# Spectral mixing with the operands swapped for modes 48 to 59

## The chip, the cores and the metric

The kernel runs on one core of a Trainium2 chip. The metric is the time of one execution on the device in microseconds. Before the change it is 430.06 us (median of 3 runs, 429.33 to 431.21). A trace of one execution is read with it; that execution took 429.86 us, with 427.9 us from its first to its last instruction.

## The reference, cut to what matters

Two stages follow each other. The first is causal attention in a sliding window of 64 over 8 batches, 8 heads, 576 positions and a head size of 64. Its output `x` has the shape 8 x 576 x 512. The second is a spectral mix:

```python
X = np.fft.rfft(x, axis=1)
Xr, Xi = np.real(X[:, :64]), np.imag(X[:, :64])
Yr = np.einsum('bmd,mde->bme', Xr, w_r) - np.einsum('bmd,mde->bme', Xi, w_i)
Yi = np.einsum('bmd,mde->bme', Xr, w_i) + np.einsum('bmd,mde->bme', Xi, w_r)
Y[:, :64] = Yr + 1j * Yi
u = x + np.fft.irfft(Y, n=576, axis=1)
return u + np.maximum(u @ w_ch, 0.0)
```

Each of the 64 modes has two weight matrices of 512 x 512 float32, 128 matrices in all. They are by far the largest input: each is 1 MB in memory.

## The kernel before, in words

**Attention** (to about 147 us in the trace) runs batch by batch. At the end of each batch a DFT by matmul (`dft`) and a turn (`dft_turn`, lines 345 to 353) put the spectrum into the tile `XQ`. Line 352 copies real and imaginary part, line 353 the negative of the imaginary part.

**Mixing** goes through 127 *halves*, numbered 0 to 126. A half is one weight matrix of one mode: real or imaginary (mode 0 has only the real one). `half(i)` does half i. The weight matrix is the standing operand: for each of four output blocks `e` and four input blocks `c`, a block of 128 x 128 weights is loaded into the array, and 16 columns of the spectrum (8 batches, real and imaginary) move past it. That is 16 matmuls of 16 columns, all on line 551:

```python
nc.tensor.matmul(out=view(psy, off + 2 * B * e, [[1, 2 * B]]),
                 lhsT=w[:, c, 128 * e:128 * e + 128],
                 rhs=XQ[:, m // HM, c, :, 1 - im:3 - im, m % HM], ...)
```

The result stands with the channels on the partitions, which is what the later stages need. Eight modes share one of two PSUM banks `psy`; after the eighth, two copies (VectorE on line 59, ScalarE on line 58) bring them to `YT` (modes 0 to 47) or `YTl` (modes 48 to 63).

**Weights** are loaded by `load_w` (line 125) from POOL's queue, 512 KB in bfloat16 each. At most eight transfers are in flight. The places for them form `ring`; `issue(i)` runs after half i and starts as many loads as `ring` and the count `places` allow. `taken` books places that other tiles need for a time, and `put(i, f, delta)` hangs a piece of work `f` behind half i and books `delta` places from there.

**The order** is written out by hand, half by half, for all compute engines. Behind halves 33 to 94 hangs the channel matmul of `x` (lines 681 to 695: transposes, `psz`, `Z0`). Behind halves 95 to 120 (from S_I = 95) hangs the inverse transform of modes 0 to 47: for each batch a turn of `YT` (`psa`, line 718, copied on line 719) and a channel matmul (`psw`, line 724, copied on line 726), then, through `first_rows` (line 733), `add_z` (`pse`, line 743) and `make_u` (`psf`, line 757), which VectorE adds to `Z0` and to `x`; and `last_tile` (`psg`). All these use float32r operands. Behind halves 120 to 124 stand five matmuls each (`psd`, line 815) whose result nobody reads. The end, after half 126, adds modes 48 to 63 (lines 882 to 922), rectifies, and stores the output.

Of the kernel before, what the change touches and what calls it, by code (L numbers as in the profile page):

```python
# [10 lines left out]
FP32R = mybir.dt.float32r  # L11
BF16 = mybir.dt.bfloat16
# [8 lines left out]
def view(ap, off, dims):  # L21

    return bass.AP(ap.tensor, ap.offset + off, [list(ap.ap[0])] + [list(d) for d in dims])
# [3 lines left out]
def kernel(  # L27
# [10 lines left out]
    nc = tc.nc  # L38
    B, H, S, D = q.shape
    NM = moe_w_r.shape[0]  # L40
# [5 lines left out]
    NC = DM // 128  # L46
# [8 lines left out]
    def evac(o, i, on_act):  # L55

        if on_act:
            return nc.scalar.copy(out=o, in_=i)  # L58
        return nc.vector.tensor_copy(out=o, in_=i)  # L59
# [5 lines left out]
    xqp = wl.enter_context(tc.tile_pool(name="xqp", bufs=1))  # L65
# [4 lines left out]
    ident_r = consts.tile([128, 128], FP32R, name="ident_r")  # L70
    trigF = consts.tile([128, NT, 2 * NM], BF16, name="trigF")
    x_sb = keep.tile([128, B // 2, 2 * NT, DM], BF16, name="x_sb")
    HM = NM // 2
    XQ = xqp.tile([128, 2, NC, B, 3, HM], BF16, name="XQ")

    def block(b, t):

# [36 lines left out]
    NLOAD = 2 * NM - 1  # L114
# [5 lines left out]
    def load_w(i, pool, tag, wt=None):  # L120
        m, im = divmod(i + (i > 0), 2)
        if wt is None:
            wt = pool.tile([128, NC, DM], BF16, name="wt", tag=tag)
        src = moe_w_i if im else moe_w_r
        nc.gpsimd.dma_start(out=wt, in_=src[m].rearrange("(p c) e -> p c e", c=NC))  # L125
        wtiles[m, im] = wt
# [28 lines left out]
    with tc.tile_pool(name="tmpf", bufs=1, side="right") as tmp:  # L155
# [6 lines left out]
        for t0, t1 in ((0, 3), (3, NT)):  # L162
            n = t1 - t0
# [14 lines left out]
    for i in range(4):  # L178
        half = i % 2
        pp = slice(64 * (i // 2), 64 * (i // 2) + 64)  # L180
        own = band[pp, half, 64 * half:64 * half + 64]
# [77 lines left out]
    for half in range(2):  # L259
        pp = slice(64 * half, 64 * half + 64)  # L260
        nc.vector.tensor_copy(out=band2[pp], in_=band[pp, half, :])
# [83 lines left out]
    def dft_turn(b):  # L345
        ps = ps_misc.tile([128, NC, 2, NM], BF16, name="pxq", tag="misc")
        for c in range(NC):
            nc.tensor.transpose(out=ps[:, c, :, :].rearrange("p r m -> p (r m)"), in_=Xs[b][:, c, :],
                                identity=ident_bf)
        for h in range(2):  # L350
            mm = slice(HM * h, HM * h + HM)
            nc.vector.tensor_copy(out=XQ[:, h, :, b, 1:3, :], in_=ps[:, :, :, mm])
            nc.scalar.mul(out=XQ[:, h, :, b, 0, :], in_=ps[:, :, 1, mm], mul=-1.0)

    nw = 0
    EARLY = LW + EW
# [42 lines left out]
    with tc.manual_schedule(engines={mybir.EngineType.PE, mybir.EngineType.Pool}):  # L399
# [11 lines left out]
        for b in range(1, B):  # L411
            start = -(-9 * (b - 1) // 2)
# [12 lines left out]

        for w in range(NWIN + 1):
            todo = [lambda b=b: dft_turn(b) for b in turns]
            turns[:] = dfts
            todo += [lambda b=b: dft(b) for b in dfts]
            dfts.clear()  # L430
            todo += [lambda b=b, j=j: unit(b, j) for b, j in sched.get(w, [])]
            n = len(todo)
# [16 lines left out]
            if w in (NWIN - 4, NWIN - 1):  # L449
                i = (B - 2) % 2 if w == NWIN - 4 else (B - 1) % 2  # L450
                spare(kTs[i])
                spare(qtp.tile([128, 4, S], BF16, name="qT"))
            if w in (NWIN - 4, NWIN):
                i = (B - 2) % 2 if w == NWIN - 4 else (B - 1) % 2
# [4 lines left out]
        for b in turns:  # L459
            dft_turn(b)  # L460
# [10 lines left out]
    MG = 8  # L471
    E0 = 96
    L0 = E0 // (2 * MG)
    R = 128 - E0
# [7 lines left out]
    YT = late.tile([128, B, NC, E0], FP32R, name="YT")  # L482
    YTl = late.tile([128, NC, B, R], FP32R, name="YTl")
# [9 lines left out]
    psys = [ps_y.tile([128, DM], FP32, name=f"psy{i}") for i in range(2)]  # L493
# [4 lines left out]
    ring.append((VT0, wlow, "wo", None))  # L498
    ring.append((2 * HM - 2, None, None, view(XQ, 0, [[DM, NC], [1, DM]])))

    Z_I = 33
    S_I = 2 * L0 * MG - 1
    T_I = NLOAD - 2
    work = {}
    taken = [0] * (NLOAD + 1)

    def put(i, f, delta=0):
        work.setdefault(i, []).append(f)
        for j in range(i, NLOAD + 1):
            taken[j] += delta  # L510

    def issue(i):
        nonlocal nw
        while nw < NLOAD:
            ring.sort(key=lambda r: (max(r[0], i), r[1] is not None, r[0]))
            if ring[0][0] > i:
                return
            if ring[0][1] is None and nw > S_I:
                first_u.append(ring.pop(0)[3])
                for j in range(i, NLOAD + 1):  # L520
                    taken[j] += 1
                continue
            held = [r[0] for r in ring if r[0] > i] + [nw]
            if any(sum(x > j for x in held) + taken[j] > places for j in range(i, nw + 1)):
                return
            _, pool, tag, ap = ring.pop(0)
            load_w(nw, pool, tag, ap)
            ring.append((nw, pool, tag, ap))
            nw += 1
# [10 lines left out]
    def give(c):  # L540
        ring.append((now, *c[1][1:]))

    def half(i):
        m, im = divmod(i + (i > 0), 2)
        w = wtiles.pop((m, im))
        psy = psys[m // MG % 2 if m < NM - 1 else 0]
        off = (m % MG) * NC * 2 * B if m < NM - 1 else 0
        own = m % MG == 0 or m == NM - 1
        for e in range(NC):
            for c in range(NC):  # L550
                nc.tensor.matmul(out=view(psy, off + 2 * B * e, [[1, 2 * B]]),  # L551
                                 lhsT=w[:, c, 128 * e:128 * e + 128],
                                 rhs=XQ[:, m // HM, c, :, 1 - im:3 - im, m % HM],
                                 start=own and not im and e == 0 and c == 0,
                                 stop=c == NC - 1 and (im == 1 or m == 0), skip_group_check=True)
        if (im or not m) and (m % MG == MG - 1 or m == NM - 2):
            g, n = m // MG, m % MG + 1
            for ri in range(2 if m < NM - 1 else 0):
                if g < L0:
                    dst = view(YT, g * 2 * MG + ri * MG, [[E0, NC], [NC * E0, B], [1, n]])  # L560
                else:
                    dst = view(YTl, (g - L0) * 2 * MG + ri * MG, [[B * R, NC], [R, B], [1, n]])
                evac(dst, view(psy, ri, [[2 * B, NC], [2, B], [NC * 2 * B, n]]), ri)

    class Parts:

# [99 lines left out]
    xts = []  # L666
# [2 lines left out]
        xts.extend(claim("xT") for _ in range(2))  # L669

    def drop_xts():
        for c in xts:
            give(c)

# [27 lines left out]
    put(Z_I, take_xts, 2)  # L702
    for k, f in enumerate(pieces):
        put(Z_I + k * (S_I - Z_I) // len(pieces), f)
    put(S_I - 1, drop_xts, -2)


    Yp, U = {}, {}
# [109 lines left out]
    with tc.manual_schedule(engines={E.PE, E.Pool, E.DVE, E.Activation}):  # L818
        with ExitStack() as pz:
            for now in range(S_I):  # L820
                if now == Z_I - 1:
                    late3 = p2.enter_context(tc.tile_pool(name="late3", bufs=1, side="right", reuse_waits="tile"))
                    Z0 = late3.tile([128, NS, 2, DM], FP32R, name="Z0")
                    ps_t = pz.enter_context(tc.tile_pool(name="ps_t", bufs=2, space=PSUM, reuse_waits="tile"))
                    ps_z = pz.enter_context(tc.tile_pool(name="ps_z", bufs=2, space=PSUM, reuse_waits="tile"))
                half(now)
                issue(now)
                if now == LW + 2:
                    nc.gpsimd.dma_start(out=wch, in_=moe_w_ch.rearrange("(c p) e -> p c e", p=128))
                if now == Z_I + 2:  # L830
                    for p in range(NP):
                        nc.gpsimd.tensor_copy(out=x_sb[64:128, p, NT - 1, :], in_=x_sb[0:64, p, NT, :])
                for f in work.get(now, []):
                    f()
        with ExitStack() as pe:
            ps_a = pe.enter_context(tc.tile_pool(name="ps_a", bufs=1, space=PSUM, reuse_waits="tile"))
            ps_e = pe.enter_context(tc.tile_pool(name="ps_e", bufs=2, space=PSUM, reuse_waits="tile"))
            for now in range(S_I, T_I):
                half(now)
                issue(now)  # L840
                for f in work.get(now, []):
                    f()
                if now >= T_I - 5:
                    psd = ps_e.tile([128, 2, DM], FP32, name="psd", tag="pse")
                    idle(psd[:, 0, :], 5)
# [48 lines left out]
        def turn(h, pw, pt):  # L894
            yl = [view(YTl, (e * B + 4 * h) * R, [[1, 128]]) for e in range(NC)]
            for e in range(NC):
                nc.tensor.matmul(out=pw, lhsT=yl[e], rhs=wch[:, e, :],
                                 start=(e == 0), stop=(e == NC - 1), skip_group_check=True)
            for e in range(NC):
                nc.tensor.transpose(out=pt[:, 128 * e:128 * e + 128].bitcast(FP32R), in_=yl[e], identity=ident_r)  # L900
# [27 lines left out]
        for k in range(6):  # L928
# [6 lines left out]
        half(T_I + 1)  # L935
        idle(bank(2, 1), 2)
        nc.vector.tensor_copy(out=view(YTl, 3 * MG - 1, [[B * R, NC], [R, B], [MG, 2]]),
                              in_=view(psys[0], 0, [[2 * B, NC], [2, B], [1, 2]]))
        turn(0, psys[1], psys[0])
        idle(bank(2, 1), 2)  # L940
        nc.scalar.copy(out=YY[0][:, 0, :], in_=psys[1])
# [55 lines left out]
```

## Time and profile before

| | |
|---|---|
| Median of 3 runs | 430.06 us (429.33 to 431.21) |
| The profiled execution | 429.86 us, span 427.9 us |
| TensorE busy | 355.8 us (83%), 5151 matmuls |
| L551, half matmuls | 1744 rows, 68.0 us busy, 192 ns each |
| VectorE, ScalarE, GpSimd busy | 199.9, 150.7, 91.4 us |
| Mean granted TensorE clock | 0.794 |
| DMA from POOL's queue | 81.80 MB, 96.0% of 16 engines' span |
| Loads of weights | 512 KB each, 19.1 us from issue to landing (median) |

A row of a matmul's duration holds its way through the array: L551's 192 ns are not 192 ns of the engine, since the next one starts some 30 ns later. "Granted clock" is the share of full speed that TensorE was given; it is 1.00 or 0.50 at any one moment. Times are from the first instruction of the trace.

### The profile page before, as it was taken

The numbers are of one execution on the slowest core, as the hardware profiler recorded it, in microseconds if no ns is written. First come the engines' busy times: TensorE is split into PE (matmuls) and PEld (weight loads), VectorE is DVE, ScalarE is ACT, GpSimd is POOL, SyncE is SP. The second block draws the span as 40 slices with busy tenths as digits, with TensorE's granted clock in tenths as the row PEclk, the third lists the DMA queues.
The fourth block names the chain that finished last, engine by engine and source line by source line (L and its number), as shares of the span: only waits on it lengthen the run. The fifth ranks groups of instructions, "written<-read, shape, count | busy, mean of one in ns | idle before, by whom it ended". The sixth has DMA issues, their size and how long they took to land.

```text
span 427.9 us, 11458 instructions
## 1 busy us (share of the span) xinstructions
PE 355.8 (83%) x5151; PEld 234.2 (55%) x5151; DVE 199.9 (47%) x364; ACT 150.7 (35%) x261; POOL 91.4 (21%) x174
## 2 busy tenths in 40 slices
PE   6989999999999675967866677696779998899993
PEld 2555765765664465855544545564555565556441
DVE  5465765865764200553334332111107557550885
ACT  3486775766863200041211120100130221200792
POOL 6131231241111313411221221221122120110000
PEclk9999998999998655795668665656666877959997
DMA  7999999999999999999999999999999999993598
GB/s 141 212 213 213 214 213 212 214 212 211 215 213 211 207 214 260 215 212 213 214 213 214 214 213 214 213 214 214 214 213 213 214 213 214 214 213 66 207 352 326
DMA packets 30352, 91.96 MB, mean 215 GB/s; under 512 B 2784, under 2 KB 2784, under 8 KB 30304
## 3 DMA queue, kind: packets, MB, share of 16 engines
q0 software_dynamic: 25344, 81.80, 96.0%
q1 hardware_dynamic: 4960, 9.44, 5.9%
q8 instruction: 40, 0.66, 0.6%
q14 instruction: 8, 0.07, 0.0%
HBM read 162.53 MB, written 9.44 MB: 402 GB/s over the span
## 4 chain that ended last, share of the span: by engine, by line
PE 51%; DMA 31%; DVE 9%; issue 4%; ACT 2%; POOL 0%; DVEq 0%; POOLq 0%; ACTq 0%
DMA wt<-in_moe_w_r_dram 18%; DMA wt<-in_moe_w_i_dram 9%; PE psy L551 7%; PE pso L318 6%; PE pst L221 6%; DMA XQ<-in_moe_w_r_dram 5%; PE psv L238 3%; PE psx L340 3%; PE pss L882 3%; PE psf L733 3%; PE psw L724 3%; DVE x_sb L326 3%; PE pss L374 2%; PE pss L891 2%; PE pss L275 2%
## 5 line engine op out<-in xcount | busy, mean ns | idle before, releaser
L551 PE MATMUL psy<-XQ,wt 128*128 128x16 bf16 x1744 | 68.0, 192 | 36.9 <-DMA wt<-in_moe_w_i_dram 18.1
L551 PEld LDWEIGHTS <-wt 128*128 128x128 bf16 x1744 | 58.8, 105 | 69.8 <-DMA wt<-in_moe_w_i_dram 28.6
L692 PE MATMUL psz<-wch,xT 128*128 128x512 f32 x144 | 61.7, 568 | 0.0
L686 DVE CAST xT<-pxt 128x1024 fp32r<-128x1024 bf16 x18 | 22.0, 1225 | 73.7 <-PE pxt L681 73.6
L695 ACT CAST Z<-psz 128x1024 fp32r<-128x1024 f32 x18 | 18.2, 1012 | 97.7 <-PE psz L692 88.4
L125 POOL DMA_DIRECT2D wt<-in_moe_w_i_dram x54 | 28.9, 536 | 91.0 <-DMA wt<-in_moe_w_i_dram 42.2
L125 POOL DMA_DIRECT2D wt<-in_moe_w_r_dram x55 | 29.8, 542 | 81.2 <-DMA wt<-in_moe_w_r_dram 36.6
L300 ACT ACTIVATE et<-pss 128x512 bf16<-128x512 f32 x72 | 39.2, 599 | 12.7 <-PE pss L294 11.6
L692 PEld LDWEIGHTS psz<-wch,xT 128*128 128x128 f32 x144 | 35.3, 271 | 5.5
L318 PE MATMUL pso<-vt,et 128*64 128x65 bf16 (+1 forms) x576 | 32.8, 205 | 4.1 <-DVE x_sb L326 3.2
L318 PEld LDWEIGHTS <-et 128*64 128x64 bf16 (+1 forms) x576 | 22.6, 110 | 15.7 <-issue 7.7
L743 DVE TENSOR_TENSOR Z<-pse,Z 128x1024 fp32r<-128x1024 f32 x16 | 19.5, 1221 | 22.9 <-PE pse L733 22.8
L326 DVE TENSOR_TENSOR x_sb<-pso,rcp 128x640 bf16<-128x640 f32 x32 | 26.3, 822 | 0.9
L275 PE MATMUL pss<-band,ident_bf 64*64 64x512 bf16 x160 | 20.5, 398 | 1.6 <-ACT et L300 1.6
L59 DVE COPY vT<-pst 128x768 bf16<-128x768 bf16 x16 | 15.3, 958 | 13.4 <-PE pst L221 13.4
L59 DVE CAST YT<-psy 128x256 fp32r<-128x256 f32 x6 | 2.5, 425 | 39.4 <-PE psy L551 39.4
L909 ACT ACTIVATE pss<-pss 128x512 f32<-128x512 f32 x35 | 18.6, 580 | 3.4 <-PE pss L891 2.7
L294 PE MATMUL pss<-qT,kT 64*64 64x128 bf16 (+1 forms) x640 | 15.6, 218 | 0.5 <-issue 0.5
L58 ACT COPY vt<-psv 128x768 bf16<-128x768 bf16 x16 | 12.9, 807 | 8.5 <-PE psv L238 8.4
L681 PE MATMUL pxt<-ident_bf,x_sb 128*128 128x128 bf16 x144 | 15.8, 278 | 0.0
L238 PE MATMUL psv<-ident_bf,vT 128*128 128x128 bf16 (+1 forms) x160 | 15.5, 226 | 0.4 <-DVE vT L59 0.4
L58 ACT COPY qT<-pst 128x768 bf16<-128x768 bf16 x16 | 12.9, 813 | 6.7 <-PE pst L221 6.7
(171 smaller groups left out, 515.2 us busy)
## 6 DMA issues: line engine op xcount, KB each, us to landing
wt<-in_moe_w_r_dram POOLq DMA_DIRECT2D x55, 512.0 KB, 19.1
wt<-in_moe_w_i_dram POOLq DMA_DIRECT2D x54, 512.0 KB, 19.1
rk<-in_k_dram POOLq DMA_DIRECT2D x8, 576.0 KB, 8.8
rq<-in_q_dram POOLq DMA_DIRECT2D x8, 576.0 KB, 12.4
rv<-in_v_dram POOLq DMA_DIRECT2D x8, 576.0 KB, 11.5
out_dram<-U SPq DMA_DIRECT2D x7, 512.0 KB, 3.4
out_dram<-x_sb SPq DMA_DIRECT2D x7, 512.0 KB, 3.7
out_dram<-x_sb SPq DMA_DIRECT2D x6, 256.0 KB, 2.6
```

The costliest lines, as they stand in the source:

```text
L58: return nc.scalar.copy(out=o, in_=i)
L125: nc.gpsimd.dma_start(out=wt, in_=src[m].rearrange("(p c) e -> p c e", c=NC))
L221: nc.tensor.transpose(out=ps[64 * hh:64 * hh + 64, c, :], in_=src[:, hh, (c0 + c) * D:(c0 + c + 1) * D], identity=ident_bf)
L238: nc.tensor.transpose(out=ps[r0:r0 + n, i, :], in_=vT[:, g, t0:t0 + n], identity=ident_bf)
L275: nc.tensor.matmul(out=pss[(2 * w + hh) % 3][64 * half:64 * half + 64, :], lhsT=ident_bf[pp, pp], rhs=view(band[pp], 128 * half, [[0, WIN ...
L300: nc.scalar.activation(out=et[:, hh, :], in_=pss[(2 * w + hh) % 3], func=ACT_F.Exp, scale=EX_SCALE)
L318: nc.tensor.matmul(out=pso[po, hh, block(b, i // 2) * VW:block(b, i // 2) * VW + D + 1], lhsT=et[pk, hh, col:col + 64], rhs=vt[pk, 1 - f % ...
L326: nc.vector.tensor_tensor(out=view(x_sb, b * NT * DM + g * D, [[4 * D, 2], [DM, NT], [1, D]]), in0=view(pso, 0, [[512, 2], [VW, NT], [1, D]]),
L551: nc.tensor.matmul(out=view(psy, off + 2 * B * e, [[1, 2 * B]]), lhsT=w[:, c, 128 * e:128 * e + 128], rhs=XQ[:, m // HM, c, :, 1 - im:3 - ...
L686: nc.vector.tensor_copy(out=o, in_=i)
L692: nc.tensor.matmul(out=psz[s][:, j, :], lhsT=xts[s % 2][0][:, j, 128 * c:128 * c + 128], rhs=wch[:, c, :], start=(c == 0), stop=(c == NC - 1))
L743: nc.vector.tensor_tensor(out=z, in0=ps, in1=z, op=ALU.add)
```

## The change

Modes 48 to 59 are halves 95 to 118. For these 24 halves the operands change places: 16 columns of the spectrum stand in the array and the weights move past, 512 columns at a time. A half is then 4 matmuls of 512 columns instead of 16 matmuls of 16. The result has batches and real/imaginary part on 16 partitions and the channels along the row. Four modes share one PSUM bank, mode j on partitions 32j to 32j + 15 (`mix_rows`). Behind the fourth, ScalarE copies the bank to `rowsum`, and after the next half's matmuls four transposes turn it (`turn_rows`), from where two copies (`to_channels`) bring it to `YTl`. Both banks are set to zero once, before mode 48.

So that 16 columns of the spectrum lie side by side, `XQ` is laid out anew: mode, then part, then batch. The copies on lines 352 and 353 write into that layout. `rowsum` is one of the two `xT` tiles, which goes back to `ring` after half 120 instead of half 94; the bookings in `put` and `issue` change with that. Modes 60 to 62 are mixed as before, in a group of their own.

```diff
-    XQ = xqp.tile([128, 2, NC, B, 3, HM], BF16, name="XQ")
+    XQ = xqp.tile([128, 2, NC, HM, 3, B], BF16, name="XQ")
...
-            nc.vector.tensor_copy(out=XQ[:, h, :, b, 1:3, :], in_=ps[:, :, :, mm])
-            nc.scalar.mul(out=XQ[:, h, :, b, 0, :], in_=ps[:, :, 1, mm], mul=-1.0)
+            nc.vector.tensor_copy(out=XQ[:, h, :, :, 1:3, b].rearrange("p c m r -> p c r m"), in_=ps[:, :, :, mm])
+            nc.scalar.mul(out=XQ[:, h, :, :, 0, b], in_=ps[:, :, 1, mm], mul=-1.0)
...
                 first_u.append(ring.pop(0)[3])
-                for j in range(i, NLOAD + 1):
-                    taken[j] += 1
                 continue
...
+    W0, WN = 48, 60
+    rowsum = []
+    due = []
+
+    def spectrum(m, c, im):
+        return XQ[:, m // HM, c, m % HM, 1 - im:3 - im, :].rearrange("p r b -> p (r b)")
+
+    def mix_rows(m, im, w):
+        j, psy = m % 4, psys[m // 4 % 2]
+        if not (j or im or m // 4 % 2):
+            for a in psys if m == W0 else ():
+                nc.vector.memset(a, 0.0)
+        for c in range(NC):
+            nc.tensor.matmul(out=psy[32 * j:32 * j + 2 * B, :], lhsT=spectrum(m, c, im), rhs=w[:, c, :],
+                             start=not im and c == 0, stop=im == 1 and c == NC - 1, skip_group_check=True)
+        turn_rows()
+        if im and j == 3:
+            nc.scalar.copy(out=rowsum[0][0][:, 0, :], in_=psy)
+            due.append(m - 3)
+
+    def turn_rows():
+        while due:
+            psa = ps_a.tile([128, NC, 128], FP32R, name="psa")
+            for e in range(NC):
+                nc.tensor.transpose(out=psa[:, e, :], in_=rowsum[0][0][:, 0, 128 * e:128 * e + 128], identity=ident_r)
+            to_channels(due.pop(), 4, lambda ri: view(psa, B * ri, [[128, NC], [1, B], [32, 4]]))
...
     def half(i):
         m, im = divmod(i + (i > 0), 2)
         w = wtiles.pop((m, im))
+        if W0 <= m < WN:
+            return mix_rows(m, im, w)
+        turn_rows()
...
-    put(S_I - 1, drop_xts, -2)
+    put(S_I - 1, drop_xts, -1)
+    put(S_I - 12, lambda: None, 1)
+    put(2 * WN, lambda: give(rowsum.pop()), -1)
```

## The prediction

> **What bounds the kernel now.** I read the chain of waits first, then the DMA issues, then busy time and clock in 2 us stretches around the changed modes. The chain (start, length, what), from half 95, where mode 48 begins:
>
> ```profile
> 294.99 20.03 DMA XQ<-in_moe_w_r_dram
> 315.07 0.66 PE psy L551 x16
> ...
> 337.06 0.49 PE psy L551 x16
> ...
> 362.86 1.84 PE psw L724 x4
> ...
> 368.22 0.98 PE psw L724 x4
> ...
> 382.15 2.13 PE psd L815 x5
> ...
> 386.54 1.08 PE psd L815 x5
> ...
> 391.63 0.49 PE psy L551 x16
> 392.12 1.51 PE pss L815 x7
> 393.63 0.48 PE psy L551 x16
> ```
>
> Half 95 starts 0.05 us after its load lands; from there the chain is TensorE's. The same work takes twice as long at times: L724 1.84 or 0.98 us, L815 2.13 or 1.08 us (0.216 us for 512 columns at full clock). L551 takes 0.49 us at either clock. The issues of the last weights on POOL, and how long the loads issued after 375 us took to land:
>
> ```profile
> 375.44 0.54 POOL L125 DMA_DIRECT2D wt<-in_moe_w_i_dram  x1 [6.33 <-PE psy L551]
> 378.22 0.53 POOL L125 DMA_DIRECT2D wt<-in_moe_w_r_dram  x1 [2.24 <-PE psy L551]
> 380.96 0.53 POOL L125 DMA_DIRECT2D wt<-in_moe_w_i_dram  x1 [2.21 <-PE psy L551]
> DMA to landing us min/median/max: 10.6/10.8/10.9
> ```
>
> The last load (half 126) lands at 391.7; its matmuls start at 393.5. Following each load's semaphore, the 30 landings after half 95's (315.02) end at 388.82, one every 2.46 us, and the page's DMA row is 9 from slice 1 to 36. So the stream sets 391.7 whatever TensorE does, unless TensorE frees tiles too late. Only 393.47 - 391.73 = 1.74 us is TensorE's own lag; it was 0.05 us at half 95, 3.2 at 119, 5.1 at 121. What follows half 126 is unchanged. Stretches (PE, PEld, DVE, ACT, POOL busy; clock; DMA):
>
> ```profile
> 328.00:330.00 2.00, 2.00 (x31) 1.48 (x28) 1.29 (x2) 0.58 (x1) 0.37 (x1) 0.50 1.04 209
> 330.00:332.00 2.00, 2.00 (x18) 1.45 (x15) 1.14 (x1) 0.00 (x0) 0.53 (x1) 0.50 1.09 219
> 336.00:338.00 2.00, 2.00 (x24) 1.38 (x23) 0.00 (x0) 1.16 (x2) 0.29 (x1) 1.00 1.06 213
> 372.00:374.00 2.00, 1.20 (x5) 0.36 (x3) 2.00 (x3) 0.00 (x0) 0.00 (x0) 1.00 1.08 219
> 378.00:380.00 2.00, 2.00 (x5) 0.78 (x6) 1.89 (x2) 0.00 (x0) 0.53 (x1) 0.50 1.05 211
> 392.00:394.00 2.00, 2.00 (x29) 1.17 (x25) 0.00 (x0) 0.00 (x0) 0.00 (x0) 1.00 0.00 0
> ```
>
> A fully busy TensorE stays at 0.50 (328 to 332, 378): busy is not enough. The clock changes at multiples of 3.41 us, so I summed what streams in each such window: moving columns, times the share of the 128 rows filled, matmuls side by side on different output columns counted once. In 122 windows, more than about 3,070 gives full clock next and less gives half, with two misses, each within 2.5%: 2,606 in 327.0 to 330.5 stays half, 3,255 in the next goes to full, 2,469 in 371.4 to 374.8 drops. An L551 half gives such a sum 256 in 0.49 us.
>
> **The change, part by part.** 24 halves (95 to 118) lose 16 matmuls of 16 columns and get 4 of 512, one after another on one group of 32 output partitions: 4 x 0.216 = 0.86 us at full clock, 1.71 at half (L815's row). Changing the array's tiling is not in this phase's trace; nearest is L238 in the attention, where a start after a change of column width comes 149 ns after the last instead of 56, and 175 on the way back: 0.1 us a side, bounds 0 and 0.35 (0.35 would leave a float32r weight load of 0.27 us, L692's PEld row, uncovered too). I take 0.2 us a half: 1.06 us at full clock, 1.9 at half, against 0.49.
>
> The other work of these halves stays: 32 L724 and 74 L733 matmuls at 0.245 us, 3 L736, 32 transposes L718 (0.28 us a group of four), plus the three new turns of four at 0.28. Sum at full clock 7.8 + 18.1 + 0.7 + 2.2 + 0.8 = 29.7 us; with 24 x 1.06 = 25.5 it is 55.2 us, where the stream gives 24 x 2.46 = 58.9. The 3.7 us left take the waits for VectorE (0.2 to 0.4 us each, 4.3 us in today's full-clock stretches; they shrink, since 0.57 us more now stands between two uses of a buffer). So at full clock TensorE just holds the stream's pace.
>
> The clock: a half now sends 2,048 columns through all 128 rows. With other work of about 2,100 a half, a window at the stream's pace holds 1.39 x 4,150 = 5,800, far over 3,070; a full window at half clock also passes (4,150 in about 4.1 us is 3,450). Half clock should last from 315 to 320 only: there 5.1 us do 1.2 halves where 2.1 arrive, a lag of 2.3 us. It stays between 2 and 4 us to half 119. Halves 119 to 126 take, at full clock, 1.5 + 2.3 + 3 x 1.57 + 2.5 + 2.0 = 13.0 us (with the fillers L815) against 17.2 of the stream; today 16.3, 8 of them at half clock. 4.2 us are made up, so half 126 starts when its load lands: 391.78 instead of 393.47, **-1.7 us**.
>
> Weight issues: the ring loses a place and keeps a tile for the turns, so the lead falls (halves between issue and use): load 112 from 10 to 6, 117 from 8 to 5, 126 from 6 to 5. At half 118 four loads are queued, 9.8 us, in which a lag up to about 6 us fits: no cost here; the price beyond it is one for one. Before half 95 the lead of 11 instead of 12 lies behind the eight transfers in flight (19.1 us over 2.46).
>
> Each turn adds an ACT copy of 128x512 (0.58 us, L719's row), issued a half earlier than it is used, and two evacuations of about 0.3 us (L937 took 268 ns). Queued behind it on ACT are Yb copies, and psa's next transposes wait for the evacuations: 0 to 0.6 us each, 1 us in all, within the 3.7. Two memsets on VectorE (under 0.7 us each, L916's row) end before 315. The copies into XQ (16 of 281 ns on VectorE, 16 of 280 on ACT) now scatter: no cost to twice as long, 4.5 us at worst in the attention, covered while transfers are queued; the thinnest place is the kT load at 140.50, which would need to be some 2 us late to leave the stream idle (it lands at 148.1; the first load of all took 5.6 us alone). I take 0.
>
> Sum: profiled time 429.86 (span 427.9 and 2.0 around it, 0.2 under the median 430.06) - 1.7, and 0.1 back towards the median: **428.3 us**.
>
> One rule speaks for a smaller cost. The Trainium skill, "TensorEngine Tiling (Array Packing)", Performance Considerations, offers the swap of operands with four column tiles for a moving side of 32 or less, up to 4x; by it a half would stream 0.22 us. Here the four matmuls of a half share a tile, and matmuls on one tile follow at 0.216 us (L815), while L318's on two halves of the columns start 4 ns apart. By that rule the sum would end at the same landing, but the slow rivals below would lose most of their price; I give it no weight.
>
> **The rivals.**
> - *A quarter tile counts a quarter for the clock.* No row here streams one 32-column tile alone. Counting 64-column tiles by their share sorts the windows nearly as well (three misses, two of them off by 5%), so it is open. Then a half gives 512; at half clock a window holds one half and 1.5 us of other work, about 1,800, and never recovers: once cold, cold to half 118. 24 halves then cost 55 + 24 x 1.9 = 101 us instead of today's 62: +39, less 4 made up and a few us of full clock before the first drop: +20 to +38, around 458 us. It decides where a tile counts less than some 0.85 of a full row. The Trainium skill, "TensorE: Matmul & The Clock Gate", What's actually happening, has the clock follow how busy the array has been in a 3.4 us window, which would clear the change of this; the busy rows at 0.50 above say that it is not so simple.
> - *Switching costs 0.35 us a side* or VectorE's waits stay: 1.56 us a half at full clock, 12 us more; lag about 12 at half 119, the short lead starves the stream, 4 made up: +4 to +9, about 436 us. For it: the margin is only 3.7 us. Against: L238's 0.1.
> - *The lag ends as today*: within 0.8 us of 430.
> - *More than the lag*: the last landing came 2.91 us after the one before instead of 2.46; if that goes too, 427.7.
>
> **How the numbers follow.** Likeliest, with the third rival: 0.63, own range 427.6 to 431.5. Quarter count 0.22, switching 0.12, more than the lag 0.03. 0.5% (2.15 us) is what a measurement here tells apart; -1.7 is near it, so 0.17 of the likeliest goes to faster. Faster 0.20, same 0.43, slower 0.37: the two slow rivals and the upper end of the first. The range reaches through the switching case into the low end of the quarter case: 427.3 to 447.
>
> **What would show it.** Right: the clock at 1.00 from about 321 to 390, the new line's matmuls at 0.216 us spacing, L815 always near 1.08 us for five, the last load landing at 391.7 and half 126 within 0.1 us of it. Wrong: 0.50 through long stretches with TensorE 2.00 busy (quarter count); clock at 1.00 but gaps of 0.3 us around each group of four (switching); POOL's last issue after 385 and the DMA row falling before 390 (lead too short); landings late before half 95 (XQ's copies).

## The result

The changed kernel takes 445.65 us, the median of six runs (440.19 to 448.73), where the kernel before took 429.69 us on the same chip (six runs, 427.74 to 431.21). The ratio is 1.032, with a 95% interval of 1.025 to 1.039: it is slower. A second set of runs gave 445.62 us and 1.038 (1.033 to 1.042). Ratios with intervals, here and below, leave out executions more than 1.5% longer than the shortest of their kernel; medians are over all. The profiled execution is the shortest of the first six, 440.19 us, with a span of 438.2 us instead of 427.9. What is read from it below is a loss of 10.3 us; what the median execution loses beyond that no profile of the changed kernel shows.

The chain of waits of the changed kernel, at the start of the swapped modes and at the last halves (start, length, what):

```profile
305.25 19.13 DMA XQ<-in_moe_w_r_dram
324.42 1.88 PE psy L556 x4
...
328.44 0.96 PE psy L556 x4
...
392.51 2.34 PE psd L852 x5
...
402.04 0.40 PE psy L581 x16
...
403.96 0.38 PE psy L581 x16
```

Half 95, the first swapped one, starts at 324.42 instead of 315.07, and half 126 at 403.96 instead of 393.63. So 9.35 of the 10.3 us were lost before the first swapped half ran. A swapped half takes 0.96 us in this chain at full clock and 1.88 at half, and the clock is full:

```profile
330.00:345.00 15.00, 13.63 (x55) 5.85 (x54) 10.11 (x9) 2.32 (x4) 3.06 (x7) 1.00 1.06 214
345.00:360.00 15.00, 14.24 (x63) 6.71 (x62) 9.42 (x9) 3.10 (x7) 1.58 (x3) 1.00 1.06 214
360.00:375.00 15.00, 13.89 (x60) 6.41 (x59) 9.29 (x10) 3.08 (x6) 2.64 (x5) 1.00 1.05 206
```

(Stretches of 15 us: busy PE, PEld, DVE, ACT, POOL; clock; DMA.) The loss lies in the attention. The page's rate in its 40 slices (10.96 us each) falls to 152, 147 and 146 GB/s in slices 12 to 14, where the kernel before has 213, 211 and 207 (first the kernel before, then the changed one):

```profile
GB/s 141 212 213 213 214 213 212 214 212 211 215 213 211 207 214 260 215 212 213 214 213 214 214 213 214 213 214 214 214 213 213 214 213 214 214 213 66 207 352 326
```
```profile
GB/s 141 212 214 213 213 212 213 212 213 214 212 152 147 146 196 212 259 213 214 214 213 213 215 214 212 214 214 212 214 214 212 214 213 214 192 211 116 187 351 326
```

The groups of the two copies into `XQ`, before and after (busy us and mean ns, then idle before them and its releaser):

```profile
L353 ACT ACTIVATE XQ<-pxq 128x128 bf16<-128x128 bf16 x16 | 4.5, 282 | 1.7 <-DVE XQ L352 1.7
...
L352 DVE COPY XQ<-pxq 128x256 bf16<-128x256 bf16 x16 | 4.3, 271 | 4.2 <-PE pxq L348 3.8 <-ACT XQ L353 0.3
```
```profile
L352 DVE COPY XQ<-pxq 128x256 bf16<-128x256 bf16 x16 | 21.0, 1315 | 6.2 <-PE pxq L348 4.1
...
L353 ACT ACTIVATE XQ<-pxq 128x128 bf16<-128x128 bf16 x16 | 12.1, 757 | 15.3 <-DVE XQ L352 15.3
```

VectorE's copy takes 1315 ns instead of 271, ScalarE's 757 instead of 282. And POOL's issue of the load that goes into a freed `kT`, the one that the prediction named as the thinnest place, before and after:

```profile
140.50 0.53 POOL L125 DMA_DIRECT2D kT<-in_moe_w_r_dram  x1 [8.22 <-PE pss L294]
```
```profile
151.91 0.53 POOL L125 DMA_DIRECT2D kT<-in_moe_w_r_dram  x1 [11.46 <-DVE XQ L352]
```

It goes out 11.4 us later. Three transfers were in flight ahead of it before, none after; it lands at 156.90 instead of 148.07, 8.8 us late, and the load of half 95 lands 9.4 us late (324.38 for 315.02). From there to the landing of half 126's load the stream takes 77.1 us instead of 76.7, and half 126 starts 2.3 us after that landing instead of 1.74: 9.36 + 0.41 + 0.56 = 10.33 us (by the matmuls' own start times, which lie some 0.16 us ahead of the chain's).

### The profile page after: what moved, and what is told of

It reads as the page before. It is cut to its first block, busy times and chain, and to the rows that moved or that the text cites. A ratio compares the mean times of both kernels' runs of the same rounds, so it can differ in the third digit from the quotient of the medians.

```text
span 438.2 us, 10900 instructions
## 1 busy us (share of the span) xinstructions
PE 357.6 (82%) x4859; PEld 223.1 (51%) x4875; DVE 216.1 (49%) x368; ACT 159.7 (36%) x266; POOL 91.2 (21%) x174
## 4 chain that ended last, share of the span: by engine, by line
PE 47%; DMA 30%; DVE 12%; issue 5%; ACT 4%; POOL 0%; DVEq 0%; POOLq 0%; ACTq 0%
DMA wt<-in_moe_w_i_dram 17%; DMA wt<-in_moe_w_r_dram 9%; PE pso L318 6%; PE pst L221 5%; PE psy L556 5%; DMA XQ<-in_moe_w_r_dram 4%; PE psy L581 4%; DVE XQ L352 3%; PE psv L238 3%; PE pss L919 3%; PE psx L340 3%; PE pss L275 2%; PE pss L928 2%; PE psw L761 2%; PE pss L374 2%
## 5 line engine op out<-in xcount | busy, mean ns | idle before, releaser
L581 PE MATMUL psy<-XQ,wt 128*128 128x16 bf16 x1376 | 47.5, 173 | 35.5 <-DMA wt<-in_moe_w_i_dram 17.6
L581 PEld LDWEIGHTS <-wt 128*128 128x128 bf16 x1376 | 42.1, 102 | 61.5 <-DMA wt<-in_moe_w_i_dram 28.7
L727 PE MATMUL psz<-wch,xT 128*128 128x512 f32 x144 | 63.3, 581 | 0.0
L318 PE MATMUL pso<-vt,et 128*64 128x65 bf16 (+1 forms) x576 | 33.9, 210 | 10.8 <-DVE x_sb L326 10.7
L326 DVE TENSOR_TENSOR x_sb<-pso,rcp 128x640 bf16<-128x640 f32 x32 | 27.9, 870 | 0.9
L275 PE MATMUL pss<-band,ident_bf 64*64 64x512 bf16 x160 | 22.7, 445 | 1.8 <-ACT et L300 1.6
L352 DVE COPY XQ<-pxq 128x256 bf16<-128x256 bf16 x16 | 21.0, 1315 | 6.2 <-PE pxq L348 4.1
L556 PE MATMUL psy<-wt,XQ 128*16 128x512 bf16 x92 | 23.7, 380 | 0.3 <-issue 0.3
L59 DVE COPY vT<-pst 128x768 bf16<-128x768 bf16 x16 | 15.3, 958 | 13.4 <-PE pst L221 13.4
L353 ACT ACTIVATE XQ<-pxq 128x128 bf16<-128x128 bf16 x16 | 12.1, 757 | 15.3 <-DVE XQ L352 15.3
L58 ACT COPY qT<-pst 128x768 bf16<-128x768 bf16 x16 | 16.5, 1040 | 1.9 <-PE pst L221 1.9
```

The source lines that it names most:

```text
L275: nc.tensor.matmul(out=pss[(2 * w + hh) % 3][64 * half:64 * half + 64, :], lhsT=ident_bf[pp, pp], rhs=view(band[pp], 128 * half, [[0, WIN ...
L318: nc.tensor.matmul(out=pso[po, hh, block(b, i // 2) * VW:block(b, i // 2) * VW + D + 1], lhsT=et[pk, hh, col:col + 64], rhs=vt[pk, 1 - f % ...
L326: nc.vector.tensor_tensor(out=view(x_sb, b * NT * DM + g * D, [[4 * D, 2], [DM, NT], [1, D]]), in0=view(pso, 0, [[512, 2], [VW, NT], [1, D]]),
L352: nc.vector.tensor_copy(out=XQ[:, h, :, :, 1:3, b].rearrange("p c m r -> p c r m"), in_=ps[:, :, :, mm])
L556: nc.tensor.matmul(out=psy[32 * j:32 * j + 2 * B, :], lhsT=spectrum(m, c, im), rhs=w[:, c, :], start=not im and c == 0, stop=im == 1 and c ...
L727: nc.tensor.matmul(out=psz[s][:, j, :], lhsT=xts[s % 2][0][:, j, 128 * c:128 * c + 128], rhs=wch[:, c, :], start=(c == 0), stop=(c == NC - 1))
```

## The experiments

**Layout or swap.** Theory A: the slow copies starve the stream of transfers. Theory B: the swapped modes cost the time. First, the new layout without the swap:

```diff
 (the kernel before)
-    XQ = xqp.tile([128, 2, NC, B, 3, HM], BF16, name="XQ")
+    XQ = xqp.tile([128, 2, NC, HM, 3, B], BF16, name="XQ")
...
+            nc.vector.tensor_copy(out=XQ[:, h, :, :, 1:3, b].rearrange("p c m r -> p c r m"), in_=ps[:, :, :, mm])
+            nc.scalar.mul(out=XQ[:, h, :, :, 0, b], in_=ps[:, :, 1, mm], mul=-1.0)
```

> The kernel before with only the spectrum's new layout (modes outside, eight images inside, so the copies L352 and L353 write elements 48 bytes apart); the mixing matmuls and the rings of the weight halves stay as they were before. Theory A (the slow copies starve the stream of transfers in the attention): the copies take 1330 and 757 ns as in the changed kernel, the stream of the weight halves comes some 9 us late, and the time is 9 to 14 us over the kernel before. Theory B (the new mixing of modes 48 to 59 costs the time, by its waits for VectorE and the shorter lead of the loads): the copies are as slow, but the late attention is caught up by the transfers, and the time is within 2 us of the kernel before.

Measured: 445.08 us (437.51 to 449.93), ratio 1.026 (1.021 to 1.032); a second set of runs gave 442.14 us and again 1.026 (1.019 to 1.033). The copies take 1315 and 757 ns again. The layout alone brings most of the loss: 12 to 15 us of 16 by the medians.

The swap without the scattered writes, in a layout where 32 modes lie side by side:

```diff
 (the changed kernel)
-    XQ = xqp.tile([128, 2, NC, HM, 3, B], BF16, name="XQ")
+    XQ = xqp.tile([128, 2, NC, 3, B, HM], BF16, name="XQ")
...
-        return XQ[:, m // HM, c, m % HM, 1 - im:3 - im, :].rearrange("p r b -> p (r b)")
+        return XQ[:, m // HM, c, 1 - im:3 - im, :, m % HM].rearrange("p r b -> p (r b)")
```

> The changed kernel with another layout of the spectrum: runs of 32 modes lie together, so that the copies write 64 bytes at a stretch, and the standing spectrum is read with one stride of 64 bytes. The mixing, its turn and the rings are those of the changed kernel. Theory A: the copies take about 0.28 us each again, the loads of the halves land as in the kernel before, and the time is that of the kernel before less 2 us to plus 2 us. Theory B: the copies are fast again, but modes 48 to 59 keep their pace of 2.9 us for each half, and the time stays 5 to 16 us over the kernel before.

Measured: 431.36 us (430.74 to 432.44), ratio 1.0033 (1.0007 to 1.0059). The two groups of copies take 271 and 282 ns in it, as in the kernel before, and half 95's load lands at 314.71. A holds for the loss; what B is left with is 1.3 us of span, taken up further down.

**Is it the copies' time, and how much is free?** In the kernel before, with its layout, the copies are only repeated:

```diff
+            for _ in range(2):                      # copies_twice; 5 in copies_long
+                nc.vector.tensor_copy(out=XQ[:, h, :, b, 1:3, :], in_=ps[:, :, :, mm])
+            for _ in range(2):                      # copies_twice; 3 in copies_long
+                nc.scalar.mul(out=XQ[:, h, :, b, 0, :], in_=ps[:, :, 1, mm], mul=-1.0)
```

> The kernel before, with each of its 16 copies L352 of VectorE and 16 negated copies L353 of ScalarE done twice in a row into the same place: 16 x 0.28 = 4.5 us more of each engine, the case that the prediction priced at nothing. Theory A with the slack of some 2 us at the load of kT as the prediction had it: 0 to 3 us over the kernel before. Theory B: no difference.

> The kernel before, with each copy L352 done five times and each negated copy L353 three times: about 1.4 us and 0.84 us for each of the 16, which is the time that the scattered copies took, without their layout. Theory A: 8 to 13 us over the kernel before, with loads of the attention going out as late as in the changed kernel. Rival A2 (the layout costs by itself, in the reads of the spectrum by the matmuls or by what writes apart cost other engines, and not by the time of the copies): under 4 us over the kernel before, while the kernel with only the layout is 9 to 14 us over it. Theory B: no difference.

Measured: twice costs nothing, 429.38 us, ratio 1.0005 (0.998 to 1.003). Long costs 439.74 us, 1.024 (1.021 to 1.027), as much as the layout alone by the intervals, and 2 to 5 us less by the medians. So the time of the copies is enough for most of the loss, and A2, which had under 4 us here, falls. It does not account for everything. These copies take 1.8 and 1.6 us more than the scattered ones, yet the load into `kT` goes out 2.4 us earlier than with the scattered layout (table below), and the six runs lie within 2.3 us of each other instead of 9 to 12. What the scattered writes add beyond their time is not shown. And a dose between: only modes 32 to 63 in the scattered layout.

```diff
 (the kernel with only the layout)
+            if h == 0:
+                nc.vector.tensor_copy(out=view(XQ, (b * 3 + 1) * HM, [[B * 3 * HM, NC], [HM, 2], [1, HM]]), in_=ps[:, :, :, mm])
+                nc.scalar.mul(out=view(XQ, b * 3 * HM, [[B * 3 * HM, NC], [1, HM]]), in_=ps[:, :, 1, mm], mul=-1.0)
+                continue
```

> The kernel before with the scattered layout for modes 32 to 63 alone; modes 0 to 31 lie as before, so 8 of the 16 copies of each engine write apart: 8 x 1.05 = 8.4 us more of VectorE and 8 x 0.48 = 3.8 us more of ScalarE. Doing each copy twice (4.5 us more of each) had cost nothing, and five and three times (18 and 9 us more) 10 us. Theory A with a slack of about 5 us in all: 1 to 4 us over the kernel before. If each scattered copy cost its own time, without slack: 6 to 7 us over it.

Measured: 428.49 us, ratio 0.9958 (0.9933 to 0.9983), a little *faster* than before; both theories missed. The load into `kT`, in the profiles in order of what the copies take, and what became of half 95:

| Kernel | More of VectorE, ScalarE (us) | `kT` load issued | lands | half 95's load lands |
|---|---|---|---|---|
| before | - | 140.50 | 148.07 | 315.02 |
| copies twice | 4.6, 4.6 | 137.22 | 148.32 | 315.18 |
| half the layout | 8.4, 3.9 | 141.93 | 148.08 | 315.03 |
| copies long | 18.5, 9.2 | 149.53 | 154.49 | 322.94 |
| layout, second profile | 16.7, 7.6 | 151.88 | 156.80 | 325.48 |
| changed | 16.7, 7.6 | 151.91 | 156.90 | 324.38 |
| changed, second profile | 16.7, 7.6 | 152.04 | 157.06 | 326.21 |

A load that goes out with little in flight lands 5.0 us later (149.53 to 154.49). The stream hence needed this one by about 143.1, and up to there lateness is free: 1.4 us late costs nothing, 9.0 late costs 6.4 at its own landing. The issue itself moves: the three kernels with the swap whose copies take what they took before (with runs, and the two built on it below) issued it between 136.97 and 141.70, and it landed between 147.95 and 148.09.

What the gain of half the layout comes from is not shown. Its late halves are shorter, 0.38 to 0.40 us in the chain against 0.45 to 0.49, since their 16 moving columns lie side by side, and in its profile half 126 starts 0.36 us after its load instead of 1.74. But shorter halves don't go with that lag. Half 126 in the chain of half the layout, of the copies done twice, and of the first profile of the kernel with only the layout:

```profile
391.86 0.38 PE psy L555 x16
```
```profile
391.94 0.48 PE psy L553 x16
```
```profile
412.35 0.38 PE psy L551 x16
```

By the matmuls' own starts the lags are 0.36, 0.41 and 1.60 us (1.48 in the second profile of the last). The second of these kernels has its late halves as long as before, the third has them short. What goes with the small lag is the clock: from the landing of half 95's load to the start of half 126 it is 0.78 and 0.80 in the first two, 0.72 and 0.75 in the profiles of the third, and 0.75 in the kernel before. Run times move with it too: on the chip of this experiment the kernel before took 427.74 us at a mean clock of 0.801 and 433.04 at 0.776.

**Why the runs spread.** The changed kernel's runs lie 8 us apart, and its profile is a short one.

> The changed kernel as it is, for a second profile: its runs spread from 440 to 449, its profile so far is of the fastest of them, and the profile of the kernel with only the layout, 8 us longer, shows a granted clock of 0.66 from 60 to 80 and from 100 to 120 us. Theory E (what the slower runs lose, they lose to the clock in the attention, before the swapped modes start): a profile of 444 or more shows stretches before 130 us at 0.6 to 0.8, where the first shows 0.91 or more, and half 95 landing later by what its span is longer, to within 2 us; from half 95 on the same pace within 2 us. Rival (the swapped modes vary): half 95 lands at 324 as in the first profile, and the difference lies behind it.

Measured: 445.62 us as the median, and 441.41 us in the profile, again the shortest of its set; neither case. Half 95's load lands 1.8 us later than in the first profile and the span is 1.2 longer. The kernel with only the layout was profiled twice, at 448.48 and at 439.92 us:

> The kernel with only the layout once more, for a second profile beside that of 448.48 us, in which the clock was 0.66 from 60 to 80 and from 100 to 120 us. Theory E (the spread is the clock in the attention): a profile under 442 shows 0.9 or more in both stretches, the load of half 95 landing earlier by as much as its span is shorter, to within 2 us; a profile over 446 shows stretches of 0.7 or less before 130 us again. Rival: the clock in the attention does not go with the span.

Stretches of 60 to 80 and 100 to 120 us, first the long execution, then the short one:

```profile
60.00:80.00 20.00, 18.32 (x276) 11.11 (x271) 10.72 (x18) 10.45 (x17) 2.52 (x4) 0.66 1.04 198
...
100.00:120.00 20.00, 19.36 (x310) 11.99 (x305) 10.35 (x18) 10.13 (x17) 3.88 (x7) 0.66 1.08 213
```
```profile
60.00:80.00 20.00, 17.43 (x345) 11.45 (x345) 13.80 (x22) 12.67 (x22) 3.77 (x6) 0.91 1.09 213
...
100.00:120.00 20.00, 17.49 (x382) 11.61 (x381) 14.12 (x23) 12.89 (x21) 1.59 (x3) 1.00 1.07 213
```

At 0.66 TensorE is busier and does a fifth fewer matmuls (586 for 727). Half 95's load lands at 333.42 and 325.48, 7.9 us apart; the spans are 446.5 and 438.1, 8.4 apart. In this pair the difference lies in the attention and goes with the clock, as theory E had it. It is one execution of each: whether the lower clock makes the delay or only comes with it is not shown, and what makes it fall was not found. I tried to hold it with fillers:

```diff
 (the kernel with only the layout)
-                mask(w + 1, max(1, 3 - n))
+                mask(w + 1, max(3, 3 - n))
```

> The kernel before with the scattered layout, and the mask's filler matmuls in the attention issued three times for every window instead of at least once. In the profile of the kernel with only the layout the granted clock fell to 0.66 over two stretches of the attention (60 to 80 and 100 to 120 us), and its runs spread from 437.5 to 449.9. Theory E (the spread is the clock: TensorE's waits for the slow copies leave stretches with too few moving columns): the fillers keep the clock at 1.00 until about 130 us, all runs lie within 4 us of each other, and the median falls to 437 to 441. Rival F (the spread comes from something else, such as the scattered writes meeting other traffic): the spread stays over 8 us, or the fillers only add their own time.

Measured: 461.45 us, 1.070 (1.065 to 1.076). The fillers brought 200 more matmuls of the mask, at some 0.4 us a row, and their own time, as F had it; the clock was 0.76 from 60 to 80 all the same. TensorE had been busy for 17.4 to 18.3 of those 20 us without them, so the dose was too large, and the run does not test E. For the changed kernel's own long runs the clock is only argued from its sister with only the layout.

**What the swap costs by itself.** In the kernel with runs, half 95's load lands 0.3 us earlier than before and that of half 126 1.7 later. POOL's issues in between:

```profile
354.89 0.53 POOL L125 DMA_DIRECT2D wt<-in_moe_w_i_dram  x1 [0.69 <-PE psy L556]
364.36 0.53 POOL L125 DMA_DIRECT2D wt<-in_moe_w_r_dram  x1 [8.94 <-PE psy L556]
```

For 9.5 us no load goes out, and four landings then come 2.6 to 3.3 us apart instead of 2.46. Theory C: the shorter ring. Theory D: VectorE's adds of `Z` and `U`, 1.2 us each in a row, for which TensorE waits. Two kernels test them; the second leaves out the addition of `x` to `U`.

```diff
 (swap_ring, on the kernel with runs)
-        rowsum.append(xts.pop())
...
+    rows_sb = view(XQ, NC * DM, [[1, DM]])          # free after mode 31, bf16
...
-    put(S_I - 1, drop_xts, -1)
-    put(S_I - 12, lambda: None, 1)
-    put(2 * WN, lambda: give(rowsum.pop()), -1)
+    put(S_I - 1, drop_xts, -2)
 (swap_u_act, on the kernel with runs)
-        nc.vector.tensor_tensor(out=U[4 * p + t], in0=ps, in1=pair_rows(p, t, 1), op=ALU.add)
+        nc.scalar.copy(out=U[4 * p + t], in_=ps)
```

> The kernel with the layout in runs of 32 modes and the swapped modes 48 to 59, with the weight ring as it was before the change: the four modes' rows are kept as bf16 in a free part of the spectrum's buffer instead of in a place of the ring, and the two bookings that shortened the lead are gone. In the kernel with runs the stream lost 1.7 us between halves 110 and 121 (steps of 2.6 to 3.3 us with one or two loads in flight) and the time was 0.33% over the kernel before. Theory C (the shorter ring lets the stream run dry): the steps stay at 2.4 to 2.5, the last load lands 1.5 to 2.5 us earlier, and the time is 0 to 0.5% under the kernel before. Theory D (waits for VectorE in the adds of Z and U set the pace, whatever the ring holds): the gain is under 0.7 us and the time stays 0.2 to 0.4% over.

> The kernel with runs, with the 16 sums U evicted by a plain copy of ScalarE in place of VectorE's addition; the addition of x is left out of U. Theory D (VectorE's adds, 1.2 us each in rows of four to six in a line, hold TensorE up): the waits for DVE at make_u are gone, the steps of the loads stay at 2.4 to 2.5 us, and the time is 1.0 to 2.5 us under the kernel with runs, that is 0.25% over to 0.3% under the kernel before. Theory C (the ring): the waits are gone, but the time moves by under 0.7 us.

Measured: the old ring 430.6 us, 1.0003 (0.998 to 1.003); `U` on ScalarE 429.78 us, 0.9982 (0.9955 to 1.0009). By the ratios that is 0.3% and 0.5% less than the kernel with runs, with intervals that overlap or just touch. With the old ring the last load lands at 391.32, 2.1 us earlier, as C had it, but half 126 starts 3.5 us later than that. With `U` on ScalarE half 126 starts 0.13 us after its load, which lands at 391.87. The time is D's, the mechanism is not: TensorE's waits for VectorE and ScalarE from 320 to 390 us come to 4.2 us, as against 4.3 in the kernel with runs, since it now waits 1.4 us for ScalarE at the sums. The clock differs too: around half 95 it is at half for 3.4 us there and for 6.8 in the kernel with runs. So the ring moves the landings, and what the adds cost is not shown. Two tries to make the swap pay: eight of the sums by TensorE and ScalarE, and fewer fillers behind the last halves, this one also in the kernel before.

```diff
 (swap_best, on swap_ring, for odd t; ScalarE then evicts)
+            nc.tensor.matmul(out=ps, lhsT=ident_bf, rhs=x_rows(b, t), start=False, stop=True)
 (swap_ring_f2 and fill2)
-                    idle(psd[:, 0, :], 5)
+                    idle(psd[:, 0, :], 2)
...
-        idle(bank(2, 1), 7)
+        idle(bank(2, 1), 3)
```

> The kernel with the old ring and rows kept apart, and in addition every second sum U (its odd tiles) gets x added by TensorE, with one matmul of the identity past x into the same bank, and is evicted by ScalarE: 8 of the 32 adds of VectorE in the stretch of the swapped modes go to ScalarE, for 16 matmuls of some 0.25 us more. Theories C and D together: the stream stays whole and the last load lands at about 391.5 us, lag at half 126 1.5 us or less, 0.3 to 0.6% under the kernel before. If only the ring mattered: as the kernel with the old ring, within 0.5 us.

> The kernel with the layout in runs, the swapped modes and the old ring, with fewer filler matmuls at the end of the loads: two in place of five behind each of halves 120 to 124, and three in place of seven ahead of half 126. In that kernel the last load landed at 391.32 us, and half 126 started only at 394.95, behind its fillers. Theory G (the fillers, run at a pace that the late halves no longer need, are the lag): half 126 starts within 0.7 us of the landing of its load, and the time is 2 to 3.3 us less, 0.4 to 0.8% under the kernel before. Rival H (the clock gives way without them): the granted clock shows 0.5 after the loads' end, and the time is the same or up to 8 us more.

> The kernel before, with the same cut of the fillers and nothing else. Half 126 started at 393.63, 1.9 us after its load landed. Theory G: the lag falls to under 0.7 us and the time by 1.0 to 1.7 us, 0.2 to 0.4% under the kernel before, so that the swap is not needed for what it could have brought. Rival H: its mixing in the old form keeps the clock at half from 375 to 385 us, the fewer fillers leave it there, the lag stays or grows, and the time is the same or up to 8 us more.

Measured: the eight sums 433.15 us, 1.005 (1.003 to 1.008), 0.5% slower: TensorE has 16 more matmuls, the last load lands at 394.65, and half 126 starts at 397.05, 2.4 us after it. The fewer fillers gave 429.16 us, 0.9985 (0.995 to 1.002), with the swap, and 428.98, 0.9973 (0.994 to 1.000), in the kernel before; neither interval is clear of 1. In both profiles half 126 starts 0.05 us after its load, as G has it, but a part of H takes much of it back. The stretch behind it in the kernel before with fewer fillers:

```profile
389.00:392.00 3.00, 1.46 (x31) 0.85 (x27) 0.00 (x0) 0.00 (x0) 0.00 (x0) 1.00 0.27 53
392.00:395.00 3.00, 3.00 (x19) 1.96 (x15) 0.27 (x1) 0.08 (x1) 0.00 (x0) 0.54 0.00 0
```

TensorE waits for the load, the clock drops, and from half 126 to the end it takes 35.7 us instead of 34.4 (36.6 in the one with the swap). Last, the changed kernel with only half of the layout scattered:

```diff
 (the changed kernel, with the copies of the kernel of half the layout)
+        if m < HM:
+            return view(XQ, (c * B * 3 + 1 - im) * HM + m, [[HM, 2], [3 * HM, B]])
```

> The changed kernel, with the scattered layout for modes 32 to 63 alone and the old one for modes 0 to 31, as in the kernel of half the layout, which lost nothing in the attention and was 0.4% faster than the kernel before. Theory A: half 95 lands within 1 us of the kernel before (315.0) and the swapped modes cost what they cost in the kernel with runs, with matmuls of the other late halves 0.1 us a half shorter: from 0.3% under to 0.4% over the kernel before. Rival: the changed kernel's shorter lead and the slower half of the copies together push the attention over its slack, 1 to 2.5% over.

Measured: 429.8 us, 1.0002 (0.997 to 1.003). Half 95's load lands at 315.62, the last one at 394.12, 2.4 us later than before, and half 126 starts 0.16 us after it. With half of the copies slow instead of all, the change costs nothing and brings nothing that these runs can tell. The best version found is the kernel before with half the layout and no swap, 0.42% faster than before (0.17 to 0.67).

## Why the prediction was wrong

The forecast was 428.3 us, a gain of 1.7 us; the medians show a loss of 16.0. The step that failed is the last term of the sum, the copies into `XQ`: "no cost to twice as long, ... I take 0". The place was right and the slack about right: `kT`'s load at 140.50, "some 2 us", where 1.4 us late is free by the runs. The bound "twice as long", for which no row stood, was not: VectorE's copy took 4.9 times as long (1315 for 271 ns) and ScalarE's 2.7 times (757 for 282). With twice, the term would have been 0, as the run with the copies doubled shows. With 16.7 and 7.6 us more the load went out 11.4 us late, and 9.4 us reached half 95. The prediction had named the sign for it: "landings late before half 95 (XQ's copies)". No row of the trace wrote single bf16 elements 48 bytes apart, and an upper end was set without one; a price for each element written was the estimate to make. One row gave a hint: L937, which the prediction quotes for evacuations, writes 64 single float32 elements, 32 bytes or more apart, in 268 ns, and L352 wrote 256 elements in 271. How the rest of the loss in the median execution, some 6 us, comes about stays open. The Trainium skill, "SBUF — State Buffer", Door 1: The DMA port swizzle, says that accesses which leave a 16-byte line each time pay a penalty; it gives no price for it, and the prediction did not use it. Here runs of 64 bytes cost what they cost before, and single elements 48 bytes apart 4.1 ns more each on VectorE ((1315 - 271) / 256) and 3.7 on ScalarE ((757 - 282) / 128), so the trace agrees that such writes are dear; whether the line or the single element is what costs, no run separates.

Point by point:
- *The clock over the swapped modes*: right. It is 1.00 from 328 to 392, after 3.4 us at half. By the prediction's sum, worked out again from the changed kernel's trace (an estimate), six windows between 324 and 386 us hold some 1,700 to 2,400 if the swapped matmuls count a quarter, and 3,300 to 5,700 if they count in full; full clock follows each of the six. The rival of the quarter count (0.22, near 458 us) falls. The median lies inside the range, but for a reason that the range was not made for.
- *0.96 us a half* at full clock in the chain, where 1.06 was forecast: right, and the rival of dear switching falls.
- *A lag of 2 to 4 us at half 119*: mis-sized. It is 4.4 us in the changed kernel and 5.1 with the old ring, where the stream stays whole. TensorE's waits for VectorE did not shrink as argued: 3.9 us before (320 to 390 us), 3.7 in the changed kernel (329 to 399 us).
- *13.0 us for halves 119 to 126*: mis-sized. It is 15.3 us in the changed kernel, 13.9 in its second profile, 15.7 with the old ring, and 13.5 with `U` taken off VectorE. In the old ring's chain the adds at 379.78 and 381.20 hold TensorE, the clock is at half from 383.2 to 386.6, and the five fillers at its start take 2.34 us:

```profile
379.78 1.23 DVE x_sb L793
...
381.20 1.14 DVE Z L779
...
383.19 2.34 PE psd L851 x5
```

- *The shorter lead is free*: wrong by a little. In the kernel with runs the stream from half 95's load to half 126's took 78.7 us instead of 76.7; with the old ring it took 76.5.
- *-1.7 us, by a lag that goes*: not reached by the swap in any run that keeps the whole computation. The lag is also less fixed than the prediction took it: the kernel before and the two with repeated copies, whose code is the same from the mixing on, show 1.74, 0.41 and 2.08 us. The stream's end, near 391.5 us in every kernel that kept it whole, and the 34.4 us behind half 126, where the fillers stayed, held as forecast.

## What to carry to other kernels

Price a changed layout at the instructions that write it, by the element and not by the instruction's shape: the same 128x256 copy took 271 ns in runs of 64 bytes and 1315 ns one element at a time. Then ask what the slower copies hold up: here buffers came free late, loads went out late, and a stream that had never stopped stood still far from the edited stage. Where the gain to be had is a lag of under 2 us at the end of such a stream, read it from several executions first: here the same late code gave 0.41 to 2.08 us.

## What the runs showed of the hardware

- A 16-column matmul with the columns side by side takes 173 ns a row (L581 of the changed kernel) and with 64 bytes between them 191 (the kernel with runs); in the chain a half of 16 takes 0.38 us instead of 0.46. The same data's copy is dearer to write that way, so reader and writer of `XQ` want opposite layouts, and half of it each way was the best of those tried (0.42%, for a reason that is not shown).
- Copies on VectorE that took 4.6 us more (copies twice) or 8.4 (half the layout) cost nothing, and 16.7 or 18.5 us more cost 9 to 10 in the profiles. There the load into `kT` went out with four and two weight loads in flight where it was free, and with none and one where it was not.
- Fewer fillers made TensorE punctual and the end slower by 1.3 us: a stretch with TensorE busy for 1.46 of 3 us was followed by one at a clock of 0.54.
- The same late code ended 0.41, 1.74 and 2.08 us behind its last load where the granted clock from half 95 on was 0.80, 0.75 and 0.72 (copies twice, the kernel before, copies long).
